# Attention with a gated two-token expert layer on one core: a new order of the first twelve blocks, and turns of small tiles moved between TensorE and the transfer queue

## The chip, the cores and the metric

The kernel runs on one core of one Trainium2 chip. The metric is the device time of one execution in microseconds (us). The time shown for the kernel before is the median of three runs. A profile is one further execution with the hardware profiler on; its span is the time from the first to the last instruction that it records.

## The reference, cut to what matters

There are 2048 tokens of 640 features. x is normalised to xn (layer norm). A 32-head attention with head size 192 runs over a window of the last 512 cached keys and values; its output is projected by wo to s. Beside it two tokens out of 2048 are chosen by a router score, sent through a gated layer, and added into their rows of xn; the result goes through silu and gates s.

```python
xn = _layernorm(x, axis=-1)
# attention: W = 512, Dh = 192, 32 heads, no grouping
q = (xn @ wq).reshape(B, Sq, Hq, Dh).transpose(0, 2, 1, 3)
scores = jnp.einsum("bhqd,bhkd->bhqk", q, k[:, :, Sk - W:]) * (Dh ** -0.5)
o = jnp.einsum("bhqk,bhkd->bhqd", _softmax(scores, axis=-1), v[:, :, Sk - W:])
s = o.transpose(0, 2, 1, 3).reshape(B, Sq, Hq * Dh) @ wo
# expert layer on the C = 2 best tokens
r = xn @ w_r
idx = jnp.argsort(-r, axis=-1)[:, :2]
y = (_silu(x_sel @ w_gate) * (x_sel @ w_up)) @ w_down * _sigmoid(r_sel)
g = _silu(xn + scatter_add(zero, idx, y))
return x + s * g
```

## The kernel before, in words

**Tiling.** Heads are taken in 8 groups of 4 (two pairs a group), tokens in four stretches of 512 (t5 = 0 to 3). A *step* is one pair of heads on one stretch; the steps run over groups, then stretches, then pairs. Each step has two *blocks* of 256 tokens, 128 blocks in all, and each block has two halves of 128 tokens. A block b is made of these tokens, which are also the words of the hand-written order:

- S.b.a, `scores` (line 358): six matmuls into a score tile of two PSUM banks (pool ps_s, two tiles, so the scores of a half need the exps of the half two before it).
- M.b.a, `row_max` (370): a VectorE reduce over the score tile.
- E.b.a, `exps` (375): two exps on ScalarE, into a ring of two blocks, then a transfer that turns p (`pT`). Line 380: blocks in SPLIT are turned in two transfers, one for each half; others in one, after the second half.
- P.b.xy, `o_item` (425): 32 matmuls of turned p with v (line 406), two reciprocals and two scalings to o_sb, one for each of two banks, on VectorE (v) or ScalarE (a) as the two letters say, then a transfer that turns o (`oT`).
- W.k, `w_item` (455): 24 matmuls of turned o with wo (line 447), then two copies or adds of the result into s_acc.
- q.i.c, `q_whole` (302): q of step i, a third c of its columns, with five matmuls and an evacuation on ScalarE (a) or VectorE (v); with a fourth number only one half of the tokens. qa and qb, `q_phase` (323), are the form in two phases that the body uses.

**Layer norm.** `first_*` (252 to 265) and `ln_parts` (486) hold the pieces of layer norm for the first stretch and the others: bn and st are VectorE statistics, sa statistics on ScalarE (`rows`, 501), dev and nw the inverse root, app and ap the application to xn on VectorE, ScalarE or GpSimd (a, v or g). turn.n (`turn_tile`, 279) transposes one 128-token tile of xn on TensorE, 5 transposes into one PSUM bank, and copies it out to xnT on ScalarE or VectorE. xT.3 (line 515) instead turns all four tiles of a stretch with one transfer.

**Loads.** x.t5, k, v, wq and wo are loads issued on SP's queue. ko (`k_order`, 118) is a GpSimd copy of keys into another order; kT (`k_transpose`, 123) is a transfer that turns them; wd (`wo_double`, 148) is a GpSimd copy of wo into the other 64 partitions, which W needs. `group_loads` (604) lays the loads of the next group into lists by block: `loads`, run at the end of a block. Lists bg, mid and end are run at other points of a block.

**Order.** All engines run in the order in which the program issues to them (a manual schedule). The first 12 blocks (HEAD = 12) follow the hand-written list FIRST (588); `first` (528) runs a token, and B.b runs all that the lists hold for block b. In the head, PSUM is two score tiles and four single banks f, which q, turns, P and W share. From block 12 to 125 each block follows BLOCK (910): A S0 M0 W m E0 B S1 M1 P E1 l, where A and B are q phases of the next step, m the list mid, P the item of two blocks before with the list bg between its halves, W the item of six before, and l the lists end and loads. The last two blocks follow LAST.

**Expert layer.** It is spread over the lists (849 to 883). The rows of the two tokens are fetched, normalised (`m_gather`, 731) to xsel, a tile of 2 x 640, and transposed on TensorE in `m_xsT` (755, block 40) to xsT, whose 32 columns are zero beyond the first two. `m_ffn` (762) runs for three parts of 512 columns: matmuls in blocks 41, 49 and 57, the gate in the next block, and `turn` (781) transposes h (128 x 128) on TensorE to hT. `m_down` (804) multiplies with w_down in blocks 62 and 68. `m_sum` (818, block 69) sums the result over partitions through DRAM, and from block 71 GpSimd adds the rows to xn (`m_add`, 831), one 128-token tile every two blocks; ScalarE and VectorE apply the gate from block 75 (`m_gate`, 840).

Of the kernel before, what the change touches and what calls it, by code (L numbers as in the profile page):

```python
# [9 lines left out]
ALU = mybir.AluOpType  # L10
# [3 lines left out]
BF16 = mybir.dt.bfloat16  # L14
# [7 lines left out]
def kernel(ctx, tc, A_x, A_k_cache, A_v_cache, A_wq, A_wo, B_x, B_w_r, B_w_gate, B_w_up, B_w_down, out):  # L22
    nc = tc.nc
    P = 128
# [131 lines left out]
    nc.sync.dma_start(out=x_in[0][:, 2, :], in_=x_v[:, 2, :])  # L156
    nc.scalar.dma_start(out=x_in[0][:, 3, :], in_=x_v[:, 3, :])
# [4 lines left out]
    for _ in range(22):  # L162
        nc.tensor.matmul(warm_ps, lhsT=idle[:, 0:P], rhs=idle, start=True, stop=True)  # L163
# [126 lines left out]
    SPLIT = (NB - 4, NB - 3, NB - 2)  # L290
# [237 lines left out]
    def first(token):  # L528
# [64 lines left out]
    S.3.0 M.3.0 turn.4.a turn.7.v S.3.1 M.3.1 turn.5.a turn.6.v E.3.0 q.2.0.a q.2.1.a P.1.va E.3.1 x.3 wd.2 wd.3 st.2.0 st.2.1 q.2.2.a st.2.2
    S.4.0 M.4.0 q.3.0.a S.4.1 E.4.0 M.4.1 st.2.3 q.3.1.a P.2.va E.4.1 st.2.4 st.2.5 st.2.6 st.2.7
    S.5.0 nw.2.0 M.5.0 q.3.2.a S.5.1 nw.2.1 nw.2.2 E.5.0 M.5.1 nw.2.3 nw.2.4 nw.2.5 nw.2.6 P.3.va E.5.1 ap.10.g ap.8.v sa.3.0.0
    S.6.0 M.6.0 E.6.0 W.0.a S.6.1 M.6.1 ap.9.v ap.11.v P.4.va E.6.1 sa.3.0.1 sa.3.2.0 st.3.6 B.6
    S.7.0 M.7.0 turn.8.v turn.11.v W.1.v turn.9.a turn.10.v S.7.1 M.7.1 E.7.0 P.5.va q.4.0.a q.4.1.a q.4.2.a E.7.1 B.7 sa.3.1.0 sa.3.2.1 st.3.7 sa.3.1.1
# [4 lines left out]
    """.split()

    def group_loads(g, b0, k0, k1, o0, t0, o1, t1, q0, q1, v0, v1, o):
        for c, at in enumerate(k0 + k1):
            loads[b0 + at].append(lambda c=c: k_piece(g, c // 2, c % 2, nc.sync))
        for pr, (a, t) in enumerate(((o0, t0), (o1, t1))):
            loads[b0 + a].append(lambda pr=pr: k_order(g, pr))
            loads[b0 + t].append(lambda pr=pr: k_transpose(g, pr))
        for c, at in enumerate(q0 + q1):  # L610
            loads[b0 + at].append(lambda c=c: wq_piece(g, c // 2, 1 + c % 2, nc.sync))
        for c, at in enumerate(v0 + v1):
            loads[b0 + at].append(lambda c=c: v_piece(g, c, nc.sync))
        for c, at in enumerate(o):
            loads[b0 + at].append(lambda c=c: wo_piece(g, c, nc.sync))
            loads[b0 + at + 2].append(lambda c=c: wo_double(g, c))
# [8 lines left out]
    M = {}  # L625
# [374 lines left out]
```

## Time and profile before

| | us |
|---|---|
| median of 3 runs (803.75 to 805.43) | 804.65 |
| the profiled execution, its own time | 802.92 |
| its span | 801.1 |
| TensorE busy in the span | 781.1 |
| VectorE busy | 589.8 |
| ScalarE busy | 530.3 |
| GpSimd busy | 309.1 |

The granted TensorE clock is 1.00 of full speed. The profile's names are PE for TensorE matmuls, PEld for its weight loads, DVE for VectorE, ACT for ScalarE, POOL for GpSimd, SP for the queue that issues most transfers. A row in the profile gives line, engine, operation and tiles, then how often; "idle before" is time in which the engine stood before such an instruction, and what ended it. Matmuls are pipelined, so the times of their rows overlap; the chain of work that ended last gives each matmul group only the time that it adds. 142.29 MB are transferred in the span, 178 GB/s in the mean, and the queue of SP takes 93.6% of the time of the 16 transfer engines.

### The profile page before, as it was taken

What the parts mean: (1) busy time and instruction counts of PE and PEld (TensorE: products, weight loads), DVE (VectorE), ACT (ScalarE), POOL (GpSimd) and SP (SyncE); (2) the same over time, 40 slices, a digit from 0 to 9 for tenths busy, and PEclk for the clock granted to TensorE, in tenths of its full rate; (3) what the DMA queues carried; (4) which work ended last, traced back from release to release, by engine and by line L of the source; (5) the groups of instructions that cost most, each with busy time, mean ns of one, the idle gap of its engine ahead of it and who ended that gap; (6) DMA issues with size and microseconds to landing.
All of it is one profiled execution on the core that took longest, in us unless ns stands there. A gap on an engine that the chain in (4) does not pass through costs nothing.

```text
span 801.1 us, 26624 instructions
## 1 busy us (share of the span) xinstructions
PE 781.1 (97%) x11354; PEld 576.6 (72%) x11354; DVE 589.8 (74%) x1086; ACT 530.3 (66%) x964; POOL 309.1 (39%) x244
## 2 busy tenths in 40 slices
PE   8799899999999999999999999999999999999997
PEld 4366577777777677777777777777777777777775
DVE  7686588887777767767666677777777777767775
ACT  5678566666666666666666667677767766666662
POOL 1312110011110101001011799949996412564865
PEclk9999999999999999999999999999999999999999
DMA  8998999799999999999998999999999899999993
GB/s 194 189 178 162 197 174 166 148 186 160 188 194 192 171 214 192 196 176 205 198 206 167 173 182 179 169 150 177 174 178 165 145 193 179 189 191 162 177 176 89
DMA packets 445112, 142.29 MB, mean 178 GB/s; under 512 B 412229, under 2 KB 444489, under 8 KB 444993
## 3 DMA queue, kind: packets, MB, share of 16 engines
q1 hardware_dynamic: 435216, 131.18, 93.6%
q10 hardware_dynamic: 8816, 6.88, 3.2%
q0 software_dynamic: 960, 2.52, 1.0%
q8 instruction: 89, 1.46, 0.8%
q14 instruction: 31, 0.25, 0.1%
HBM read 39.98 MB, written 2.62 MB: 53 GB/s over the span
## 4 chain that ended last, share of the span: by engine, by line
PE 89%; DMA 4%; DVE 3%; ACT 2%; issue 1%; POOL 0%; SPq 0%; DVEq 0%; ACTq 0%; POOLq 0%
PE w L447 24%; PE q_ps L340 22%; PE o_ps L406 20%; PE s L367 19%; DMA pT<-pexp 2%; PE q_ps L309 2%; ACT pexp L377 1%; DVE nm L372 1%; PE warm_ps L163 1%; DMA xnT<-xn 1%; DMA wo_g<-in_A_wo_dram 1%; ACT o_sb L420 0%; ACT qT L315 0%; DVE fin_o L475 0%; ACT qT L352 0%
## 5 line engine op out<-in xcount | busy, mean ns | idle before, releaser
L372 DVE TENSOR_REDUCE nm<-s 128x2 f32<-128x1024 f32 x256 | 313.1, 1224 | 135.0 <-PE s L367 130.7
L377 ACT ACTIVATE pexp<-s,nm 128x512 bf16<-128x512 f32 x512 | 324.1, 689 | 96.5 <-DVE nm L372 61.1
L340 PE MATMUL q_ps<-xnT,wq_g 64*128 64x512 bf16 (+1 forms) x2340 | 232.3, 323 | 3.4 <-DMA xnT<-xn 1.5
L447 PE MATMUL w<-wo_g,oT 64*128 64x320 bf16 x3072 | 231.0, 296 | 0.8 <-ACT o_sb L420 0.8
L367 PE MATMUL s<-kT,qT 64*128 64x512 bf16 x1536 | 211.6, 376 | 5.0 <-ACT pexp L377 3.9
L447 PEld LDWEIGHTS <-oT 64*128 64x128 bf16 x3072 | 170.9, 94 | 58.4 <-issue 0.9
L406 PEld LDWEIGHTS <-pT 64*128 64x128 bf16 x4096 | 178.7, 94 | 28.9 <-issue 2.4
L406 PE MATMUL o_ps<-v_sb,pT 64*128 64x193 bf16 x4096 | 197.1, 243 | 0.1
L420 ACT ACTIVATE o_sb<-o_ps,rl 128x192 bf16<-128x192 f32 x256 | 93.8, 418 | 136.7 <-DVE rl L413 132.8
L340 PEld LDWEIGHTS <-wq_g 64*128 64x128 bf16 x2340 | 126.7, 100 | 49.0 <-issue 2.7
L151 POOL COPY wo_g<-wo_g 64x1920 bf16<-64x1920 bf16 x32 | 58.0, 1817 | 219.0 <-DMA wo_g<-in_A_wo_dram 208.2
L367 PEld LDWEIGHTS <-qT 64*128 64x128 bf16 x1536 | 85.1, 94 | 60.1 <-issue 6.4
L470 DVE TENSOR_TENSOR s_acc<-s_acc,w 128x320 f32<-128x320 f32 x192 | 85.0, 484 | 32.4 <-PE w L447 32.3
L352 ACT ACTIVATE qT<-q_ps 128x1024 bf16<-128x1024 f32 x114 | 92.4, 811 | 5.3
L121 POOL COPY k_perm<-k_raw 128x768 bf16<-128x768 bf16 x30 | 25.0, 851 | 139.6 <-DMA k_raw<-in_A_k_cache_dram 108.1
L417 DVE TENSOR_TENSOR o_sb<-o_ps,rl 128x384 bf16<-128x384 f32 x128 | 71.4, 558 | 4.7 <-DVE rl L413 0.4
L836 POOL TENSOR_SCALAR yh<-y_bc,oh 128x640 bf16<-128x640 bf16 x32 | 61.9, 1933 | 3.9 <-DMA y_bc<-y_d 2.3
L837 POOL TENSOR_TENSOR xn<-xn,yh 128x640 bf16<-128x640 bf16 x32 | 44.7, 1397 | 2.7
L413 DVE RECIPROCAL rl<-o_ps 128x2 f32<-128x2 f32 x256 | 30.3, 160 | 16.3 <-PE o_ps L406 9.4
L901 POOL TENSOR_TENSOR s_acc<-s_acc,x_fin 128x640 f32<-128x640 f32 x16 | 22.4, 1399 | 32.0 <-DMA x_fin<-in_A_x_dram 31.5
L833 POOL TENSOR_SCALAR xn<-xn 128x640 bf16<-128x640 bf16 x16 | 29.4, 1838 | 0.8
L478 POOL TENSOR_TENSOR fin_o<-fin_t,s_acc 128x640 bf16<-128x640 f32 x12 | 18.5, 1540 | 17.6 <-DVE fin_t L473 11.0
(138 smaller groups left out, 258.4 us busy)
## 6 DMA issues: line engine op xcount, KB each, us to landing
wo_g<-in_A_wo_dram SPq DMA_DIRECT2D x32, 240.0 KB, 4.2
k_raw<-in_A_k_cache_dram SPq DMA_DIRECT2D x32, 192.0 KB, 3.4
v_sb<-in_A_v_cache_dram SPq DMA_DIRECT2D x32, 192.0 KB, 4.2
wq_g<-in_A_wq_dram SPq DMA_DIRECT2D x14, 288.0 KB, 3.9
wq_g<-in_A_wq_dram SPq DMA_DIRECT2D x14, 192.0 KB, 3.7
x_fin<-in_A_x_dram SPq DMA_DIRECT2D x16, 160.0 KB, 3.5
pT<-pexp SPq DMA_TRANSPOSE x130, 4.8
oT<-o_sb SPq DMA_TRANSPOSE x126, 3.5
```

Source lines behind the costliest of these rows:

```text
L151: nc.gpsimd.tensor_copy(out=grp[g][("wo", pr)][half(1), cs, :], in_=grp[g][("wo", pr)][half(0), cs, :])
L340: mm = nc.tensor.matmul(q_ps[k][:, 0:n] if type(q_ps) is list else q_ps[:, k, 0:n], lhsT=wq[half(r), dc, c:2 * Dh:3], rhs=xnT[half(r), tok ...
L352: nc.scalar.activation(out=out, in_=q_ps[:, :, 0:n], func=ACT.Copy, scale=scale)
L367: nc.tensor.matmul(s_of[b, a][:, r, :], lhsT=qT_of[i][half(r), c, u * P:(u + 1) * P], rhs=grp[g][("kT", pr)][half(r), :, c, :], start=(c = ...
L372: rm = nc.vector.tensor_reduce(out=nm_of[b, a], in_=s_of[b, a], axis=AX.X, op=ALU.max, negate=True)
L377: nc.scalar.activation(out=p_ring[:, b % 2, a, :, hh, :].rearrange("p (x j) e -> p x j e", x=2), in_=s_of[b, a][:, hh, :].rearrange("p (j ...
L406: nc.tensor.matmul(o_of[b][r][:, a, 0:Dh + 1], lhsT=pT_ring[half(r), b % RP, a, k, :], rhs=v_ring[half(r), (g * PAIRS + pr) % RV, k, 0:Dh ...
L417: nc.vector.tensor_tensor(out=o_sb, in0=src, in1=rl[:, r].unsqueeze(2).unsqueeze(3).to_broadcast([P, 2, 3, HK]), op=ALU.mult)
L420: nc.scalar.activation(out=o_sb[:, a], in_=src[:, a], func=ACT.Copy, scale=rl[:, r, a:a + 1])
L447: nc.tensor.matmul(w_ps[r][:, 0:HD], lhsT=oT_ring[half(r), bs[pr] % RT, c, :], rhs=grp[g][("wo", pr)][half(r), c, cs], start=(pr == 0 and ...
L470: nc.vector.tensor_tensor(out=acc, in0=acc, in1=src, op=ALU.add)
L836: nc.gpsimd.tensor_scalar(out=yh, in0=M["y_bc"][:, j, :], scalar1=M["oh"][:, n, j:j + 1], scalar2=None, op0=ALU.mult)
```

## The change

The list FIRST is replaced, and what it names is widened:

- Tile 3 of x goes on SP's queue, not ScalarE's; 13 warm-up matmuls in place of 22.
- The p of blocks 0 to 3 is turned in two transfers each.
- The loads of the second group that fall into the first 12 blocks are tokens of the list of their own (gk keys, go their order, gT their turn, gq, gv, gw loads of wq, v, wo, gd the double); `group_loads` keeps those of block 12 and later. One load of wo moves from block 13 to 14, with its double from 15 to 16.
- xT.3 goes; tiles 12 to 15 are turned on TensorE (turn.12 to turn.15).
- xsel is a tile of 32 x 640, zeroed once, and is turned by a transfer to xsT, issued at the end of block 40; h is turned by a transfer at the end of blocks 43, 50 and 58. The first m_ffn moves from block 41 to 42, the second half of the w_down loads by one block, m_down(1) from 68 to 69 and m_sum from 69 to 70.

```diff
-    nc.sync.dma_start(out=x_in[0][:, 2, :], in_=x_v[:, 2, :])
-    nc.scalar.dma_start(out=x_in[0][:, 3, :], in_=x_v[:, 3, :])
+    for n in (2, 3):
+        nc.sync.dma_start(out=x_in[0][:, n, :], in_=x_v[:, n, :])
...
-    for _ in range(22):
+    for _ in range(13):
         nc.tensor.matmul(warm_ps, lhsT=idle[:, 0:P], rhs=idle, start=True, stop=True)
...
-    SPLIT = (NB - 4, NB - 3, NB - 2)
+    SPLIT = (0, 1, 2, 3, NB - 4, NB - 3, NB - 2)
...
+        elif op == "gk":
+            k_piece(1, n[0] // 2, n[0] % 2, nc.sync)
+        elif op == "go":
+            k_order(1, n[0])
+        elif op == "gT":
+            k_transpose(1, n[0])
...
     FIRST = """
-    bn.1.0 x.1.0 bn.0.0 bn.0.1 v.0 v.1 dev.0 bn.1.1 dev.1 app.0 turn.0.a app.1 bn.3.0 turn.1.a bn.2.0 bn.2.1 dev.2 bn.3.1 kturn.av k.1.0 k.1.1 ko.1 wq.1 x.1.1 dev.3 exp st.1.0 q.0.0.0.v app.2 q.0.1.0.a kT.1 app.3 q.0.2.0.a turn.2.v turn.3.a st.1.1
...
+    v.0 x.1.0 bn.0.0 bn.1.0 x.1.1 bn.1.1 dev.1 bn.0.1 app.1 dev.0 k.1.0 app.0 bn.2.0 turn.0.a bn.3.0 bn.3.1 turn.1.a v.1 kturn.av bn.2.1 wq.1 dev.3 q.0.2.0.a k.1.1 q.0.0.0.v dev.2 v.2 q.0.1.0.a
+    ko.1 app.2 app.3 st.1.0
+    S.0.0 M.0.0 exp x.2 turn.2.a turn.3.a S.0.1 kT.1 M.0.1 st.1.1 E.0.0 st.1.2 wo.0 q.0.1.1.a q.0.0.1.a q.0.2.1.v E.0.1
+    S.1.0 wo.1 st.1.3 st.1.4 S.1.1 M.1.0 st.1.5 E.1.0 q.1.1.a M.1.1 q.1.2.a E.1.1 st.1.6 q.1.0.v st.1.7 nw.1.0
+    S.2.0 nw.1.1 nw.1.2 M.2.0 wo.2 S.2.1 nw.1.3 nw.1.4 nw.1.5 M.2.1 nw.1.6 st.2.0 E.2.0 ap.7.g ap.6.v P.0.vv E.2.1
+    S.3.0 M.3.0 ap.4.a v.3 S.3.1 turn.6.a ap.5.g wd.0 turn.5.a turn.4.v turn.7.v E.3.0 st.2.1 st.2.2 P.1.va M.3.1 wo.3 st.2.3 E.3.1 q.2.1.a q.2.2.v st.2.4 wd.1 q.2.0.v P.2.va
+    S.4.0 M.4.0 S.4.1 E.4.0 x.3 M.4.1 st.2.5 q.3.1.a E.4.1 wd.2 st.2.6 st.2.7 nw.2.0 q.3.2.a nw.2.1 nw.2.2
+    S.5.0 M.5.0 nw.2.3 E.5.0 nw.2.4 q.3.0.v S.5.1 wd.3 nw.2.5 sa.3.0.0 nw.2.6 M.5.1 E.5.1 sa.3.2.0 W.0.v ap.10.g
+    S.6.0 ap.11.g M.6.0 gk.0 E.6.0 ap.9.g ap.8.v W.1.v P.3.av S.6.1 M.6.1 P.4.va
+    S.7.0 st.3.6 E.6.1 turn.10.v turn.11.v turn.9.a turn.8.v sa.3.0.1 M.7.0 S.7.1 E.7.0 gk.1 q.4.2.v gq.0 q.4.1.v q.4.0.a
+    qa.5.0.1 sa.3.1.0
+    S.8.0 M.7.1 go.0 E.7.1 st.3.7 gw.0 sa.3.2.1 sa.3.1.1 nw.3.0 nw.3.1 M.8.0 W.2.v qb.5.0.1 nw.3.2 nw.3.3 nw.3.4 nw.3.5 P.5.av S.8.1 M.8.1 gq.1 nw.3.6 E.8.0 E.8.1 P.6.va ap.15.v
+    qa.5.2 ap.12.v
+    S.9.0 S.9.1 M.9.0 ap.14.g turn.12.v turn.14.v E.9.0 ap.13.g qb.5.2 turn.13.v M.9.1 turn.15.v
+    S.10.0 gT.0 E.9.1 gk.2 gk.3 P.7.vv W.3.v M.10.0 E.10.0 S.10.1 gv.0 P.8.vv W.4.a
+    qa.6.0.1 M.10.1 gd.0
+    S.11.0 E.10.1 M.11.0 B.11 go.1 E.11.0 W.5.v qb.6.0.1 P.9.av q.6.2.v S.11.1 M.11.1 E.11.1 gw.1 gv.1
...
-            group_loads(1, 0, (6, 6), (9, 9), 7, 10, 11, 14, (8, 9), (12, 13), (10, 11), (16, 17), (8, 11, 13, 15))
+            group_loads(1, 0, (6, 6), (9, 9), 7, 10, 10, 14, (8, 9), (12, 13), (10, 11), (16, 17), (8, 11, 14, 15))
...
-        nc.gpsimd.memset(M["xsT"], 0.0)
+        M["xsel"] = M["s"].tile([32, D], BF16, name="xsel")
+        nc.gpsimd.memset(M["xsel"], 0.0)
...
     def m_xsT():
-        xsT_ps = f_tile([P, DC, 2], BF16, "xsT_ps")
-        for dc in range(DC):
-            nc.tensor.transpose(out=xsT_ps[:, dc, :], in_=M["xsel"][:, dc * P:(dc + 1) * P], identity=ident[0:2, 0:2])
-        nc.vector.tensor_copy(out=M["xsT"][:, :, 0:2], in_=xsT_ps)
+        nc.sync.dma_start_transpose(out=M["xsT"], in_=M["xsel"])
...
         def turn():
-            h_ps = f_tile([P, P], BF16, "h_ps")
-            nc.tensor.transpose(out=h_ps, in_=M["h"], identity=ident)
-            nc.vector.tensor_copy(out=M["hT"][:, fb * 4:(fb + 1) * 4, :].rearrange("p c t -> p (c t)"), in_=h_ps)
+            nc.sync.dma_start_transpose(out=M["hT"][:, fb * 4:(fb + 1) * 4, :].rearrange("p c t -> p (c t)"), in_=M["h"])
...
-    bg[40].append(m_xsT)
+    loads[40].append(m_xsT)
...
-    for fb, km in enumerate((41, 49, 57)):
+    for fb, km in enumerate((42, 49, 57)):
...
-        bg[km + 1].append(turn)
+        loads[km + 1].append(turn)
...
-            loads[a + 5 * h].append(m_wd_piece(h, q))
+            loads[a + 6 * h].append(m_wd_piece(h, q))
...
-    bg[68].append(m_down(1))
-    bg[69].append(m_sum)
+    bg[69].append(m_down(1))
+    bg[70].append(m_sum)
```

More of the change, by code (lines that the diff above doesn't have):

```diff
@@ L593 @@
[L593 to L597, printed above, removed]
@@ L607, in group_loads, with at @@
-        for pr, (a, t) in enumerate(((o0, t0), (o1, t1))):
[L608 to L616, printed above, removed]
+        def at(b, f):
+            if b0 + b >= HEAD:
+                loads[b0 + b].append(f)
```

31 lines of the change are left out of this document (20 added, 11 removed).

## The prediction

> **What bounds the kernel now.** I read the busy times and slices first, then windows of the first 12 blocks, TensorE's waits, and the chain that ended last.
>
> ```profile
> PE 781.1 (97%) x11354; PEld 576.6 (72%) x11354; DVE 589.8 (74%) x1086; ACT 530.3 (66%) x964; POOL 309.1 (39%) x244
> ...
> PE   8799899999999999999999999999999999999997
> DMA  8998999799999999999998999999999899999993
> ```
>
> TensorE is full from slice 6 on, so nothing that only rearranges work after about 110 us can pay; what can pay is the head (slices 1 to 5) and TensorE work taken out of the body. The transfer engines are nearly full too, so a transfer's place in SP's queue matters. Busy time by stage (us, then PE, PEld, DVE, ACT, POOL, clock, DMA share, GB/s):
>
> ```profile
> 0.00:39.05 39.05, 31.09 (x253) 16.68 (x254) 27.48 (x67) 23.40 (x44) 7.69 (x13) 1.00 0.93 190
> 39.05:90.05 51.00, 47.09 (x606) 30.01 (x606) 37.13 (x77) 37.49 (x80) 11.04 (x20) 1.00 0.92 179
> 90.05:108.11 18.06, 17.23 (x232) 12.57 (x233) 12.41 (x22) 10.40 (x19) 4.37 (x10) 1.00 1.13 182
> ```
>
> 39.05 is the end of S.4.0 (scores of block 4, first half); at 90.05 block 12 begins on TensorE. What TensorE waited for (total, times, longest):
>
> ```profile
> PE s L367 <- ACT pexp L377: 3.9, 5, 1.0
> PE q_ps L340 <- DMA xnT<-xn: 1.5, 1, 1.5
> PE q_ps L309 <- DVE xnT L283: 1.4, 1, 1.4
> PE tp L282 <- DVE xn L193: 1.3, 1, 1.3
> ...
> PE xsT_ps L758 <- DVE xsel L752: 0.5, 1, 0.5
> ```
>
> Scores wait for exps, which sit in ScalarE's queue behind evacuations of q; that is what a new order can mend. The chain shows one transfer of the head the change deletes, and one delayed behind it:
>
> ```profile
> 74.59 6.92 DMA xnT<-xn
> ...
> 88.34 7.00 DMA pT<-pexp
> ```
>
> **Body, -2.1 us.** In the chain, w's products start every 5.90 us, except around the turns on TensorE:
>
> ```profile
> 253.24 1.64 PE w L447 x24
> 259.14 1.66 PE w L447 x24
> 266.28 1.63 PE w L447 x24
> 272.95 1.63 PE w L447 x24
> 279.13 1.63 PE w L447 x24
> ```
>
> 259.14 to 266.28 is 7.14: 1.24 over 5.90, for xsT with its wait. 272.95 to 279.13 is 6.18: 0.28 for one h turn, and 321.21 to 327.39 and 369.48 to 375.66 give the same. All four go: 1.24 + 3 x 0.28 = 2.1. (The 6.67 between is m_ffn's matmuls, which stay.) The four replacements go on SP behind that block's pT. SP's slot for an o turn is 1.24, and its gap there, 270.2 to 272.25, covers it. No trace row has a 32x640 or 128x128 turn; landing lies between the shortest (3.0, a pT) and longest pT (9.3). I take the pT median, because it waits in the same queue:
>
> ```profile
> pT<-pexp SPq DMA_TRANSPOSE x130, 4.8
> oT<-o_sb SPq DMA_TRANSPOSE x126, 3.5
> ```
>
> Issued at 268.9, xsT lands at 273.7; m_ffn's first product, now a block later, is due near 276.1. Median: hidden. At 9.3 it would cost 2.1, all of this gain. h has 4 blocks or more. m_sum, one block later, shifts y_bc by 5.9; GpSimd finishes tile 0 at 459.6 and ScalarE reads it at 474.7, so 9.2 remains: nothing. The wd loads move with m_down, nothing. The xsel memset on GpSimd, between one and four times the 0.25 row (32x640 has four times the elements per row), has no reader for 28 blocks.
>
> The Trainium skill, "DMA: Bandwidth & Descriptors", section "Rules for kernel authors", says a transfer under 64 KB is mostly overhead and should be coalesced; h is 32 KB. By that rule the turns cost SP and the queues out of proportion to their bytes. No run here shows a turn that small; the sum would still be the same while TensorE does not wait.
>
> **Head, to S.0.0, -0.8.** First transposes start at 8.31, when 22 warm-up matmuls end; their tile was ready at 6.7. Thirteen end near 6.1 (ten at 0.43, three at 0.21). The new order has its first two tiles ready near 7.2 and turns tile 0 then. x tile 3 changes from ScalarE's queue to SP's, 1.5 us later; DVE has other stats first, 0 to -0.6 us of this gain. I take -0.8.
>
> **Head, to S.4.0, +0.6 by itself, but P.2 is then done.** The new order also moves work between engines. Counted over the new list, VectorE gains 3 xnT copies (0.48), 7 whole q evacuations and 3 second halves of o (0.56), and loses 4 applies (0.46). A 128x512 q evacuation on VectorE is in no row: 128x256 takes 0.425, the 128x1024 reduce 1.22, so between these; a 128x384 scaling takes 0.56, 0.13 for 128 elements more, so I take 0.69. Net 1.4 + 4.8 + 1.7 - 1.8 = **+6.1 on VectorE**. ScalarE gains one copy (0.70), loses 7 q (0.60) and 3 o (0.73): **-5.7**. GpSimd gains 4 applies (0.87), idle there. TensorE gains 20 transposes for tiles 12 to 15 (0.06 each): +1.2.
>
> I walked the list by hand with row durations, each instruction when its engine and its inputs are free. So: S.0.0 at 11.9; VectorE, behind app.3 and st.1.0, runs M.0.0 13.0 to 14.2; ScalarE, behind the table and two tile copies, E.0.0 14.7 to 15.9 (was 15.67), q's two evacuations, E.0.1 16.9 to 18.1. VectorE, behind q.0.2.1 and st.1.3 and st.1.4, M.1.0 18.1 to 19.3, and E.1.0 follows at 19.4 (21.37). In the same way E.1.1 at 22.0 (22.99), E.2.0 25.3 (24.94; six small VectorE steps and q.1.0 stand ahead), E.3.0 31.3 (31.10), E.3.1 35.0 (36.85). P.2 needs the bank of q.2.1, which ScalarE empties after E.3.1, at 36.9; P.2 ends at 38.5, S.4.0 at 39.2 (39.05). The transfers give a later bound: x.2 (640 KB) now goes out near 12.6 instead of 26.4, ahead of kT.1 and P.0's turns. The bytes queued up to pT of block 2 are some 6.9 MB; at 189 GB/s that is 36.3, from a start near 2: P.2 from 38.3, S.4.0 at 40.3. I take the middle, 39.7. pT of blocks 0 to 3 in halves adds a slot each:
>
> ```profile
> L383 SPq DMA_TRANSPOSE pT<-pexp x124: 1316/2502/5739, 18.8 to 762.6; - x124
> L381 SPq DMA_TRANSPOSE pT<-pexp x6: 1232/1517/2148, 766.1 to 777.8; - x6
> ```
>
> At 1.5 each SP issues 1.5 + 1.5 + 1.24 + 0.63 = 4.9 us a block against some 6: hidden, and the first half leaves an exp pair (1.27) earlier.
>
> **Head, from S.4.0 to block 12.** TensorE's least work, at chain durations: before, 15 S x 0.65 + 8 P x 1.35 + 6 W x 1.63 + 12 q x 1.08 + 4 tile turns x 0.3 (0.29 in the chain) = 44.5; taken, 89.37 - 39.05 = 50.3, so 5.8 lost, then 0.7 until 90.05. After: one P less, four turns more, 44.4. Lost of the 5.8: xnT's transfer 1.7 goes; the rest I keep, since ScalarE's relief and VectorE's load nearly cancel: 4.1. Bounds: 0 and 15 (each of 16 reduces held 0.69 more). Block 12 begins at 39.7 + 44.4 + 4.1 = 88.2: **-1.85**. The group-1 loads keep their deadlines: k's turn stays in block 10, wo and v come for block 16.
>
> **After block 12.** P.12 was at 108.11, where 90.05 + 5.1 + 2 x 5.9 = 106.95 was possible: 1.2 lost, and 0.7 before. The chain names pT of block 10 (88.34, landing 7.00 later), held behind xnT, k and wq. Now E.10.1 falls near 82, its transfer lands before 90, and S.11.1 covers q.6.2's evacuation. I take half: **-0.9**, bounds 0 and -1.9.
>
> **Sum.** -1.85 - 0.9 - 2.1 = -4.8 (the -0.8 is the walk's start, so inside the first). Span 801.1 becomes 796.3; 1.8 lies around it (802.92 - 801.1), so 798.1 profiled; the median shown is 1.7 above that execution: **799.9**.
>
> **Rivals.**
> *VectorE takes ScalarE's place (slower).* In blocks 4 to 11, reduces of VectorE now stand behind q evacuations and xnT copies; each delays exp, then the scores two ahead, as only two score tiles exist. For: +6.1 us on the engine that is busier over the first 90 us (64.6 against 60.9). Against: VectorE idled 17.1 us before reduces there. Price 0.69 a reduce; the 4.8 gain is eaten by the seventh of 16 and the tenth makes it slower by 0.2%. At twelve: 799.9 + 8.3 = 808.
>
> *Transfers bind early.* For: DMA share 0.93 up to 39.05. x.2's 640 KB, 3.5 us, holds kT.1 and P.0 wholly; 1.1 less than the walk is already taken: +2.4, 802.3.
>
> *The clock falls.* The rows show it rise after 4.3 us of warm-up (weights every 0.43, then ten in 2.04):
>
> ```profile
> 5.43 0.15 PEld L163 LDWEIGHTS <-idle 128*128 128x128 bf16 x1 [0.28 <-issue]
> 5.77 2.04 PEld L163 LDWEIGHTS <-idle 128*128 128x128 bf16 x10 [0.19 <-issue]
> ```
>
> Thirteen leave 0.6 us after it, then a thin stretch; if it fell until the scores, 4.4 us of PE work (0.72 + 0.83 + 1.80 + 1.01) doubles, about half beside copies: +2.2, 802.1. The Trainium skill, "TensorE: Matmul & The Clock Gate", section "Part 1: The HAM clock gate", has the clock halve after an idle window of some 3.4 us and calls the window free-running; the longest gap I see coming is 1.2. Granted clock is 1.00 throughout before.
>
> *The turns do not leave the path.* xsT lands late by the 2.1 above: 802.0.
>
> *The order fits better.* L of 1 instead of 4.1, and all 1.9 after block 12: -4.1, 795.8.
>
> **Chances.** Forecast (797.5 to 802.5) 0.42, better fit 0.16, VectorE 0.22, the three of 802 together 0.20. About 0.2%, 1.6 us, is what a measurement of this kernel can tell from no change: faster is below 803.0, slower above 806.3. The forecast and better fit are faster, and half of the three (0.10): 0.68. Same: their other half and 0.04 of VectorE, 0.14. Slower: 0.18. Range 795.0 to 806.5: it leaves out the best 0.05 and VectorE's worst 0.15.
>
> **What would show it.** Body right: w spacing 5.90 near block 40, no wait for xsT or hT. Head right: block 12's first q at 88.2 (85 to 91), no xnT transfer in the chain, E.3.1 near 35. VectorE rival: scores waiting for pexp and pexp for nm, VectorE unbroken from 60 to 90. Transfers: P.0 or S.2.0 waiting for pT or kT. Clock: under 1.00 before 14 us. The forecast is wrong if block 12 begins after 93.

## The result, and the profile after

| | before | after |
|---|---|---|
| median of 4 runs each | 804.86 us (803.75 to 805.43) | 795.67 us (794.27 to 796.98) |
| ratio after to before, 95% interval | | 0.9887 (0.9867 to 0.9908) |
| the profiled execution, its span | 802.92, 801.1 | 796.98, 795.1 |

The changed kernel is faster by 9.2 us, 1.1%. That lies inside the range of the prediction (795.0 to 806.5), at its lower end; the forecast of 799.9 had 4.8 us of gain. The two profiled executions are 6.0 apart, less than the medians, because the one of before was below all four runs of its table row and the one of after was the highest of its own. So the traces here account for 6.0 us, and the other 3 is taken up with the experiments.

The page of the kernel after, busy times and slices:

```profile
PE 779.8 (98%) x11357; PEld 576.6 (73%) x11357; DVE 597.6 (75%) x1091; ACT 525.9 (66%) x952; POOL 313.8 (39%) x248
...
PE   8899999999999999999999999999999999999997
DMA  9989999799999999999999999999999899999993
```

VectorE went up by 7.8 (6.1 was forecast; some of the 7.8 is steps that stand still, below), ScalarE down by 4.4 (5.7). In TensorE's row slice 2 went from 7 to 8 tenths and slice 5 from 8 to 9, and only the first two slices are below 9 until the last. Two of the three stretches of before, with the columns us, then PE, PEld, DVE, ACT, POOL, clock, DMA share, GB/s:

```profile
0.00:39.05 39.05, 32.60 (x285) 18.05 (x286) 31.52 (x76) 23.39 (x43) 9.58 (x14) 1.00 1.01 215
39.05:90.05 51.00, 50.38 (x645) 32.69 (x645) 42.09 (x84) 35.97 (x73) 15.86 (x30) 1.00 0.93 168
```

From 39.05 to 90.05 TensorE idles 0.6 us where it idled 3.9, and VectorE is busy 42.1 of the 51 without anybody losing by it. (The second stretch after holds almost a block more than before, since block 12 begins in it.) The first stretch moves 215 GB/s where it moved 190. TensorE's own timeline (start, us, instructions of one line in a row) gives the steps of the head, here S.0.0, S.4 and the first q of block 12:

```profile
10.82 1.11 PE L367 MATMUL s<-kT,qT 64*128 64x512 bf16 x6
...
36.83 1.53 PE L367 MATMUL s<-kT,qT 64*128 64x512 bf16 x12
...
84.82 1.26 PE L340 MATMUL q_ps<-xnT,wq_g 64*128 64x512 bf16 x10
```

The row at 36.83 holds both halves of block 4's scores, so S.4.0 ends near 37.5. Block 12 begins at 84.82; before it began at 90.05. And its waits (total, times, longest):

```profile
PE s L367 <- ACT pexp L377: 2.2, 4, 0.8
PE w L447 <- ACT o_sb L420: 2.1, 3, 0.8
...
PE o_ps L406 <- DMA v_sb<-in_A_v_cache_dram: 0.8, 1, 0.8
```

The wait for xnT's transfer (1.5) is gone, scores wait 2.2 for exps instead of 3.9, and a line that was smaller is now second: W waiting for o_sb. Two of those three waits (0.68 and 0.76) are in the blocks whose work was moved, below.

**Where the time went.** The w products are a clock of the kernel: from block 12 on there is one each block. The one of block 13 starts at 92.47 where it started at 98.85, 6.4 us earlier. From there to the end of the span it takes 702.6 where it took 702.3. So the head gained 6.4, more than twice the 2.75 of the prediction, and the body, which was to gain 2.1, gained nothing. These are the rows of w in the chain of work that ended last, of the kernel after, in the blocks whose work was moved:

```profile
252.71 1.66 PE w L447 x24
...
259.29 1.81 PE w L447 x24
...
265.37 1.63 PE w L447 x24
...
272.03 1.67 PE w L447 x24
...
278.72 1.81 PE w L447 x24
```

265.37 to 272.03 is 6.66, m_ffn's products, one block later than before. But 252.71 to 259.29 is 6.58 and 272.03 to 278.72 is 6.69, in place of 5.90 each. No turn runs on TensorE in them any more. (The chain starts such a row where its own part begins; by TensorE's timeline the two spacings are 6.75 and 6.85.) What ran in them is told by the timelines of GpSimd and VectorE:

```profile
255.31 1.78 POOL L151 COPY wo_g<-wo_g 64x1920 bf16<-64x1920 bf16 x1 [18.62 <-DMA wo_g<-in_A_wo_dram]
255.34 1.93 DVE L774 TENSOR_SCALAR xsel<-xg,rs 2x640 bf16<-2x640 bf16 x1
...
274.43 1.78 POOL L151 COPY wo_g<-wo_g 64x1920 bf16<-64x1920 bf16 x1 [11.54 <-DMA wo_g<-in_A_wo_dram]
274.50 1.86 DVE L797 SCALAR_TENSOR_TENSOR th<-th 128x128 f32<-128x128 f32 x1
```

A 2 x 640 scaling takes 1.93 us, and a step on 128 x 128 numbers 1.86. Each begins just after a 1.78 us copy of GpSimd (wo_double) has begun, and ends within 0.2 us of it: 257.27 behind 257.09, 276.36 behind 276.21. Behind them, in the program's order, stand the next reduce, its exp, and the scaling of o that W needs. And the same was there before the change, one instruction earlier. Kernel before, same views:

```profile
261.39 1.78 POOL L151 COPY wo_g<-wo_g 64x1920 bf16<-64x1920 bf16 x1 [17.90 <-DMA wo_g<-in_A_wo_dram]
261.60 1.58 DVE L197 SCALAR_TENSOR_TENSOR rs<-mv,rs 2x1 f32<-2x1 f32 x1
```

Two numbers take 1.58 us. The same kind of step takes 0.14 where no copy runs beside it. So the 7.14 between 259.14 and 266.28, which the prediction put down to the turn of xsT and its wait, may have been mostly this.

### The profile page after: what moved, and what is told of

It reads as the page before. It is cut to its first block, busy times and chain, and to the rows that moved or that the text cites. A ratio compares the mean times of both kernels' runs of the same rounds, so it can differ in the third digit from the quotient of the medians.

```text
span 795.1 us, 26635 instructions
## 1 busy us (share of the span) xinstructions
PE 779.8 (98%) x11357; PEld 576.6 (73%) x11357; DVE 597.6 (75%) x1091; ACT 525.9 (66%) x952; POOL 313.8 (39%) x248
## 3 DMA queue, kind: packets, MB, share of 16 engines
q10 hardware_dynamic: 8672, 6.72, 3.5%
## 4 chain that ended last, share of the span: by engine, by line
PE 89%; DVE 5%; ACT 3%; DMA 2%; issue 1%; SPq 0%; DVEq 0%; ACTq 0%
PE w L447 25%; PE q_ps L340 23%; PE o_ps L406 20%; PE s L367 19%; DVE nm L372 1%; ACT pexp L377 1%; DMA pT<-pexp 1%; PE q_ps L309 1%; DMA v_sb<-in_A_v_cache_dram 1%; ACT o_sb L420 0%; DVE s_acc L470 0%; ACT xnT L283 0%; DMA x_in<-in_A_x_dram 0%; PE tp L282 0%; PE gu_ps L787 0%
## 5 line engine op out<-in xcount | busy, mean ns | idle before, releaser
L420 ACT ACTIVATE o_sb<-o_ps,rl 128x192 bf16<-128x192 f32 x250 | 91.7, 418 | 134.8 <-DVE rl L413 129.5
L417 DVE TENSOR_TENSOR o_sb<-o_ps,rl 128x384 bf16<-128x384 f32 x131 | 73.1, 558 | 4.5
```

The lines of the kernel that those rows point to most:

```text
L417: nc.vector.tensor_tensor(out=o_sb, in0=src, in1=rl[:, r].unsqueeze(2).unsqueeze(3).to_broadcast([P, 2, 3, HK]), op=ALU.mult)
L420: nc.scalar.activation(out=o_sb[:, a], in_=src[:, a], func=ACT.Copy, scale=rl[:, r, a:a + 1])
```

## The experiments

Two theories stood at first. **A**: all of the gain is the head's. The body's turns were cheap, most of the 1.24 was the VectorE step that stands still beside a GpSimd copy, and after the change other steps stand still in the same way. **B**: the body gained its 2.1 as forecast, the head the rest, and the flat sum of the body is another disturbance. Beside these stood theories of what in the head had paid: the shorter warm-up, the turns on TensorE, the halved turns of p, the exchange of evacuations between engines, or only the order. Every ratio is to the kernel before, run beside it on the same chip (medians of before 804.64, 803.98 and 803.64 in the three sets).

### The two halves of the change apart

**e1**: the kernel after, with the expert layer of before.

```diff
-        nc.sync.dma_start_transpose(out=M["xsT"], in_=M["xsel"])
+        xsT_ps = f_tile([P, DC, 2], BF16, "xsT_ps")
+        for dc in range(DC):
+            nc.tensor.transpose(out=xsT_ps[:, dc, :], in_=M["xsel"][:, dc * P:(dc + 1) * P], identity=ident[0:2, 0:2])
+        nc.vector.tensor_copy(out=M["xsT"][:, :, 0:2], in_=xsT_ps)
...
-    for fb, km in enumerate((42, 49, 57)):
+    for fb, km in enumerate((41, 49, 57)):
...
-        loads[km + 1].append(turn)
+        bg[km + 1].append(turn)
```

> The head of the changed kernel (new list, 13 warm-up matmuls, halves of p, tiles 12 to 15 turned on TensorE) with the expert layer of the kernel before (turns of xsel and h on TensorE, m_ffn first in block 41). Theory A: the whole gain is the head's, 6.4 us between the two profiles at P.12, plus what the medians add (9.2 in all); the turns of xsel and h, moved to transfers, give nothing, because two VectorE instructions then run against a GpSimd copy. A expects this kernel within 1 us of the changed one, about 795.7, and the block of the xsel turn 7.1 long again. Rival B: the turns give their 2.1 us and the profile of the changed kernel was an unlucky execution; B expects 797.8.

**e2**: the kernel before, with the expert layer of after; the same edit the other way round.

```diff
-    bg[40].append(m_xsT)
+    loads[40].append(m_xsT)
...
-    for fb, km in enumerate((41, 49, 57)):
+    for fb, km in enumerate((42, 49, 57)):
...
-        bg[km + 1].append(turn)
+        loads[km + 1].append(turn)
```

> The head of the kernel before with the expert layer of the changed kernel (xsel and h turned by transfers, m_ffn first in block 42, m_down and m_sum a block later). Theory A expects no gain, 804 to 805.5; rival B expects 2.1 less than the kernel before, 802.8. Under A a w product waits for o_sb on ScalarE once or twice near blocks 40 to 43, 0.7 us each, behind a VectorE instruction that takes 1.5 to 2 us in place of 0.3 to 0.45.

**e3** and **e4** are the kernels after and before once more, unchanged, for the scatter.

> The changed kernel itself, for a second profile of it beside the others. Both theories: a median of 795.7 within 1 us. Under A, w starts more than 6.6 us apart in block 41 and in block 44 again, each with a VectorE instruction stretched beside a GpSimd copy; under B they are 5.90 apart except for the 6.67 of m_ffn.

> The kernel before itself, for a second profile. Both: a median of 804.9 within 1 us. Under A the small VectorE step before xsel, or xsel itself, is again stretched to 1 us or more by the GpSimd copy of wo, and block 41 of w is about 7.1 long; if the stretch is absent, the turn with its wait should cost about 0.4 in place of 1.24.

| | median us | ratio (95%) | w of block 13 at |
|---|---|---|---|
| e1, head alone | 798.32 | 0.9913 (0.9881 to 0.9945) | 92.20 |
| e2, body alone | 805.83 | 1.0019 (0.9994 to 1.0043) | 98.34 |
| e3, after | 796.60 | 0.9898 (0.9868 to 0.9927) | 92.19 |
| e4, before | 804.87 | 0.9988 (0.9968 to 1.0008) | 99.91 |

The body's edits alone gain nothing: e2 is not faster than before, and its trace has the xsel step at 1.85 us beside a copy of GpSimd. e4 has the stretch of before again: the 2x1 step takes 1.61, and the spacing is 7.16. The head alone gains 6.3 us of 804.64, and its w of block 13 is as early as that of e3. By time e1 is 1.7 slower than e3: A expected it within 1 us of the kernel after, and it came near the 797.8 of B. But most of the two intervals is common to both, so that the times alone don't decide.

The traces do. From w of block 40 to w of block 59 the body's gain of 2.1 would leave 114.4 of the 116.51 of before. It took 116.52 after, 116.25 in e3, and 116.00 in e1, which has the old expert layer. So e1 is not slower than e3 there; it is 1.0 slower ahead of block 40 and 1.6 slower behind block 72, where the two do the same work. And in e1 the copy came after the xsel step and not beside it (timelines of VectorE, GpSimd and TensorE):

```profile
255.90 0.43 DVE L774 TENSOR_SCALAR xsel<-xg,rs 2x640 bf16<-2x640 bf16 x1
256.45 1.78 POOL L151 COPY wo_g<-wo_g 64x1920 bf16<-64x1920 bf16 x1 [19.00 <-DMA wo_g<-in_A_wo_dram]
257.24 0.27 PE L780 MATMUL xsT_ps<-ident,xsel 2*128 2x2 bf16 x5
```

The scaling takes 0.43, xsT's five matmuls wait for nothing, and the spacing of w there is 6.23: the turn of xsT on TensorE costs 0.33 by itself. The same work cost 1.23 in the kernel before; so 0.9 of the 1.24 was the stretched step. e14 (below), with the expert layer of before, agrees: its copy begins at 264.52, behind the 2x1 step (0.14) and xsel (0.43), and its spacing is 6.22. In e3 the copy misses xsel as well, catches h (1.76 us), and one spacing is 6.74. In e2 a step of h begins 0.90 us into the copy of 279.23 and takes 1.02 in place of 0.28: what it pays is the rest of the copy. Which step is caught changes from execution to execution, since the copy starts when its load lands.

### Taking away the copies that collide

**e5**: the kernel after, with the two doubles of wo in question made by a second load from DRAM instead of GpSimd's copy. It adds two transfers and takes two copies away.

```diff
+        if (g, c) in TWICE:
+            eng.dma_start(out=grp[g][("wo", pr)][half(1), cs, :], in_=wo_v[:, c0 + cs.start:c0 + cs.stop, :])
+
+    TWICE = ((3, 0), (3, 1))
...
+        if (g, c) in TWICE:
+            return
```

> The changed kernel, in which the first two wo pieces of group 3 are loaded twice (into both halves of the partitions) in place of being copied by GpSimd; so no GpSimd copy runs beside xsel and the two steps to h. Theory A (the body's gain was eaten because a VectorE instruction stands still while the GpSimd copy of wo runs): xsel takes 0.43 and both steps to h 0.3 each in the profile, w is 5.90 apart in blocks 41 and 44, and the time falls by 0.9 to 1.8 from the changed kernel's 796.6, to about 795.3. Rival C (the stretch comes from something else, such as the transfer of wo landing): the same instructions are stretched again, or W waits as before, and the two extra loads cost 0 to 1 us: 796 to 797.5.

799.32, ratio 0.9942 (0.9922 to 0.9961), where after had 0.9887 and 0.9898: it gave part of the gain back. Yet the steps are as A says once no copy runs, and the waits in the blocks behind them are others (VectorE's, TensorE's and SP's timelines of e5, whose lines are numbered 6 higher):

```profile
255.16 0.43 DVE L780 TENSOR_SCALAR xsel<-xg,rs 2x640 bf16<-2x640 bf16 x1
274.10 0.28 DVE L803 SCALAR_TENSOR_TENSOR th<-th 128x128 f32<-128x128 f32 x1
...
273.73 5.18 SPq L389 DMA_TRANSPOSE pT<-pexp  x1
...
282.00 1.52 PE L412 MATMUL o_ps<-v_sb,pT 64*128 64x193 bf16 x32 [1.09 <-DMA pT<-pexp]
...
284.86 1.26 SPq L807 DMA_TRANSPOSE hT<-h  x1
```

0.43 and 0.28: the cause of the stretch is shown. But P now waits for its turned p, 1.09 and 0.69 us in these blocks (and 1.37 in the head), and the w spacings here are 8.11 and 7.26. The p of the first wait is the one issued at 273.73: its issue holds SP for 5.18 us, where the same turn takes 3.17 in the kernel after, and the next turn of p can only leave behind it, at 281.03. hT's turn is issued at 284.86, after both, so it is not their cause. The two added loads are not needed for it either: e8, e9 and e10 below, whose copies miss all these steps, hold SP for 4.42, 5.36 and 4.44 at the same turn, and so does e13 (4.43), which turns this h on TensorE. All five turn xsT on SP 8 to 9 us earlier. e1 and e14 turn it on TensorE and have 3.13 and 2.30; but e3 and e7 turn it on SP and have 3.07 and 3.58. So xsT's slot may be what makes p late, and it isn't shown. A's time (a gain over after) failed. The collision can't be priced by taking the copy away; its price is the 0.9 from e1 and e14.

### Which part of the head paid

**e7**: the kernel after, but the last stretch of xn is turned by one transfer, as before.

```diff
-    S.9.0 S.9.1 M.9.0 ap.14.g turn.12.v turn.14.v E.9.0 ap.13.g qb.5.2 turn.13.v M.9.1 turn.15.v
+    S.9.0 S.9.1 M.9.0 ap.14.g E.9.0 ap.13.g xT.3 qb.5.2 M.9.1
```

> The changed kernel with tiles 12 to 15 of xn turned by one transfer again, as before (xT.3 behind the last of their applies). Theory D (the transfer of xnT and the p transfers queued behind it cost the old head some 2 to 3 us): block 12 begins 1.5 to 3 later than in the changed kernel, with a wait of q for the xnT transfer, and the time is 798 to 799.5. Rival E (the gain is all from the order of exps and evacuations; the transfer's 7 us are hidden where it now stands): within 1 us, and 1.2 us less TensorE work and 1.9 us less VectorE work even make it 0.5 faster.

802.18, ratio 0.9986 (0.9958 to 1.0013): nearly all of the gain is gone. Block 12 begins at 86.64 and w of block 13 at 94.85, 2.4 later than after. TensorE's waits in e7:

```profile
PE q_ps L340 <- DMA xnT<-xn: 1.6, 1, 1.6
```

The 1.6 is the wait that the turns removed. 2.4 of the head's 6.4 hang on them, as theory D had it. The median lost some 6 us, more than the head's 2.4, and the rest isn't explained: the profiled execution took 807.67, 5.5 above the median, and P waits 3.26 in it for a turned p in one place of the body, at 462.97 (the spacing is 11.01). e12, e13 and e14, with other edits, have a long spacing in the same blocks, 72 and 73 (8.32, 9.58 and 7.35), so no link with the edit of e7 is shown.

**e9**: the kernel after with 22 warm-up matmuls.

```diff
-    for _ in range(13):
+    for _ in range(22):
```

> The changed kernel with 22 warm-up matmuls in place of 13. If the shorter warm-up is worth what the start of the scores moved beyond the tile order, 0.8 to 0.9: the first transposes start at 8.3 in place of 7.2, the first scores near 11.7 in place of 10.8, and the time is 0.5 to 1.0 higher, 797.3. If later waits absorb it: within 0.3. The clock at the start should be the same in both.

798.54, ratio 0.9933 (0.9912 to 0.9953). S.0.0 begins at 12.32, 1.50 later, block 12 at 86.38 and w of block 13 at 94.02, both 1.55 later. In the new order the start of the head passes on whole. Of the 1.5, 0.6 is this execution's: its 22 matmuls took 7.72 us and those of before 7.12 (why, below), so that the nine matmuls themselves are worth about 0.9.

**e12**: the same edit in the kernel before, 13 matmuls for 22.

```diff
-    for _ in range(22):
+    for _ in range(13):
```

> The kernel before with 13 warm-up matmuls and nothing else changed. In the changed kernel the nine matmuls were worth 1.5 us at the sixth w product. Theory G (a start earlier by as much moves the whole head): first transposes at 7.3 in place of 8.3, and block 12 0.8 to 1.5 earlier than 90.05; time 803.3 to 804. Rival (the old head's later waits, on the xnT transfer above all, absorb it): block 12 within 0.4, time 804.6.

806.78, ratio 1.0032 (1.0015 to 1.0049): not faster, even a little slower. TensorE's timeline shows where the earlier start ends:

```profile
6.75 1.01 PE L282 MATMUL tp<-ident,xn 128*128 128x128 bf16 x10 [0.21 <-DVE xn L264]
...
11.67 1.01 PE L282 MATMUL tp<-ident,xn 128*128 128x128 bf16 x10 [1.29 <-DVE xn L264]
12.61 1.47 PE L367 MATMUL s<-kT,qT 64*128 64x512 bf16 x12
```

The first tiles are turned 1.4 us earlier (6.75 for 8.14), but in the old order the turns of tiles 2 and 3 stand ahead of S.0.0 and wait 1.29 for VectorE; S.0.0 begins at 12.61 where it began at 12.68. The new order puts S.0.0 ahead of them. So theory G failed. That the whole became slower by 2.6 us isn't explained by the head: its w of block 13 is at 98.72 (before 98.85). The trace has longer spacings in the body (8.32 at 461.75, 6.72 at 509.79); what ties them to the edit stays open.

**e14**: the kernel before with the turns of tiles 12 to 15 on TensorE in place of the transfer.

```diff
-    qa.5.0.1 S.8.0 B.8 nw.3.0 M.8.0 nw.3.1 nw.3.2 W.2.v qb.5.0.1 nw.3.3 S.8.1 M.8.1 E.8.0 nw.3.4 nw.3.5 nw.3.6 P.6.va E.8.1 ap.13.a ap.15.g ap.14.v ap.12.v xT.3
-    qa.5.2 S.9.0 M.9.0 B.9 W.3.v E.9.0 qb.5.2 S.9.1 M.9.1 P.7.va E.9.1
+    qa.5.0.1 S.8.0 B.8 nw.3.0 M.8.0 nw.3.1 nw.3.2 W.2.v qb.5.0.1 nw.3.3 S.8.1 M.8.1 E.8.0 nw.3.4 nw.3.5 nw.3.6 P.6.va E.8.1 ap.13.a ap.15.g ap.14.v ap.12.v
+    qa.5.2 S.9.0 M.9.0 turn.12.v turn.14.v B.9 W.3.v E.9.0 turn.13.v qb.5.2 turn.15.v S.9.1 M.9.1 P.7.va E.9.1
```

> The kernel before with tiles 12 to 15 turned on TensorE (copies on VectorE, in block 9) in place of the transfer, and nothing else changed. Theory D: block 12 and the sixth w product 2.4 us earlier, as the changed kernel with the transfer put back was 2.4 later; time 802.2, and after block 12 no wait of exps for the turned p of block 10. If the order has to change too for the turns to pay: less than 1 us.

807.11, ratio 1.0044 (1.0023 to 1.0066), slower. The transfer's wait is gone, but the turns come in a place where TensorE waits three times between 71 and 77 us: 0.5 and 0.5 ahead of the turns, for VectorE, and 0.8 where W of step 3 needs a bank that VectorE still has to empty:

```profile
74.07 2.19 PE L447 MATMUL w<-wo_g,oT 64*128 64x320 bf16 x24 [0.79 <-DVE xnT L283]
```

Block 12 begins at 92.98 (before 90.05), w of block 13 at 100.62 (98.85). Of the 1.8, 0.6 is there at the first transposes (8.74 for 8.14; a longer warm-up again). So the same edit that is worth 2.4 in the new order costs about 1.2 in the old one.

**e10**: the kernel after, with all the q evacuations from block 1 on that it had put on VectorE given to ScalarE.

```diff
-    S.1.0 wo.1 st.1.3 st.1.4 S.1.1 M.1.0 st.1.5 E.1.0 q.1.1.a M.1.1 q.1.2.a E.1.1 st.1.6 q.1.0.v st.1.7 nw.1.0
+    S.1.0 wo.1 st.1.3 st.1.4 S.1.1 M.1.0 st.1.5 E.1.0 q.1.1.a M.1.1 q.1.2.a E.1.1 st.1.6 q.1.0.a st.1.7 nw.1.0
...
-    S.3.0 M.3.0 ap.4.a v.3 S.3.1 turn.6.a ap.5.g wd.0 turn.5.a turn.4.v turn.7.v E.3.0 st.2.1 st.2.2 P.1.va M.3.1 wo.3 st.2.3 E.3.1 q.2.1.a q.2.2.v st.2.4 wd.1 q.2.0.v P.2.va
+    S.3.0 M.3.0 ap.4.a v.3 S.3.1 turn.6.a ap.5.g wd.0 turn.5.a turn.4.v turn.7.v E.3.0 st.2.1 st.2.2 P.1.va M.3.1 wo.3 st.2.3 E.3.1 q.2.1.a q.2.2.a st.2.4 wd.1 q.2.0.a P.2.va
...
-    S.7.0 st.3.6 E.6.1 turn.10.v turn.11.v turn.9.a turn.8.v sa.3.0.1 M.7.0 S.7.1 E.7.0 gk.1 q.4.2.v gq.0 q.4.1.v q.4.0.a
+    S.7.0 st.3.6 E.6.1 turn.10.v turn.11.v turn.9.a turn.8.v sa.3.0.1 M.7.0 S.7.1 E.7.0 gk.1 q.4.2.a gq.0 q.4.1.a q.4.0.a
```

(q.3.0 and q.6.2 as well.)

> The changed kernel with its seven whole q evacuations of the head that VectorE does (steps 1 to 6) given back to ScalarE, in the same places of the list: VectorE loses 4.8 us in the first 12 blocks, ScalarE gains 4.2. Theory F (the relief of ScalarE is what shortens the head, since exps stood behind q): block 12 begins 1.5 to 4 later and the time is 798 to 800.5. Rival (VectorE is now the tighter engine, and the evacuations hold up its reduces): block 12 begins 1 to 3 earlier, 794 to 796. In between, within 0.7, the split does not matter, and the order of the other tokens does.

797.05, ratio 0.9920 (0.9899 to 0.9941); block 12 at 85.08 and w of block 13 at 92.72, 0.25 later than after; S.0.0 began 0.5 later already (11.31), ahead of the edit. Which of the two engines empties q hardly matters.

**e8**: the kernel after, p of blocks 0 to 3 turned in one transfer each.

```diff
-    SPLIT = (0, 1, 2, 3, NB - 4, NB - 3, NB - 2)
+    SPLIT = (NB - 4, NB - 3, NB - 2)
```

> The changed kernel with p of blocks 0 to 3 turned in one transfer each, as before. If the halves matter (P.0, P.1 and P.2 of the changed kernel already wait up to 0.8 for a transfer each): P.0 starts 1 to 2 later, S.4.0 and block 12 follow by 0.5 to 2, time 797.5 to 799. If four more slots of SP cost as much as they give: block 12 begins within 0.3 of 84.8 and the time is within 0.7 of the changed kernel's 796.6.

797.28, ratio 0.9915 (0.9886 to 0.9945); w of block 13 at 93.00, 0.5 later, from an S.0.0 that began 0.2 earlier (10.59). So the halves are worth 0.5 to 0.8 in the head, below what the times can tell.

### A version that might beat both

**e13**: the kernel after, with xsel made at the end of block 40, the gate of the first m_ffn a block later, the first h turned on TensorE again, and v of the fourth head loaded a block earlier.

```diff
-            spot(29 + b).append(it)
+            (end[40] if b == 11 else spot(29 + b)).append(it)
...
-        mid[km + 1].append(act)
-        loads[km + 1].append(turn)
+        mid[km + (2 if fb == 0 else 1)].append(act)
+        (bg[km + 2] if fb == 0 else loads[km + 1]).append(turn)
```

> The changed kernel with three moves away from what it was seen to wait for: the making of xsel goes to the end of block 40 and the gate of the first m_ffn to block 44 (both out of the GpSimd copy of wo), the first h is turned on TensorE in block 44 (0.27) since SP's slots of blocks 43 to 46 are full, and the load of v for head 3 goes one block earlier (P.2 waited 0.8 for it). If these waits are what ate the body's gain: no small VectorE step stretched, blocks 40 to 47 at 5.90 but for 0.77 of m_ffn and 0.3 of the turn, and the time 0.8 to 2 below the changed kernel, 794.6 to 795.8. If the transfers of p run late there for another reason: blocks 45 and 46 lose 1 us or more again, and the time is 796 to 798.

797.42, ratio 0.9891 (0.9862 to 0.9920): not to be told from after. The edits did what they say: no VectorE step is stretched, the 0.8 us wait for v is gone, and w of block 13 is at 91.36, 1.1 earlier than after. The profiled execution, the slowest of its six (800.37), gave it back in the body: spacings of 7.14 (282.81) and 6.31 (289.12) around the turn of h, which waits 0.90 for a bank that ScalarE empties late, its exps having waited 2.29 for the late turn of p, and 9.58 at 462.79, where P waits 3.02 for its turned p.

## Why the prediction was right, and where its sizes were wrong

**Sign and range** were right; 9.2 us were gained where 4.8 were forecast. What came is the split of no rival: 6.4 from the head and nothing from the body, where the sum had 2.75 and 2.1, and "The order fits better" 6.9 and 2.1. That the median lies beside the 795.8 of that rival is luck: it has 792.2 for the span (796.3 - 4.1), the profiled one is 795.1, and the difference is made up by the 3 us that the medians show beyond the two traces.

A second pair of executions, e4 and e3, has these 3 us: their spans differ by 9.3, 7.7 up to w of block 13 and 1.6 behind it (704.3 and 702.7). But executions of the old head differ among themselves: w of block 13 is at 98.34 (e2), 98.85 (before) and 99.91 (e4), and the first transposes at 7.76, 8.14 and 8.88. Most of that is the warm-up. Its weights are loaded every 0.43 us at first and every 0.20 later, the change comes at 4.96 in e2, 5.77 in before and about 7.1 in e4, and so the 22 matmuls take 6.74, 7.12 and 7.85:

```profile
1.19 7.85 PE L163 MATMUL warm_ps<-idle 128*128 128x512 bf16 x22 [1.19 <-DVE idle L160]
```

In the new head 13 of them end before the first tile is ready, and w of block 13 lies between 92.19 and 92.47 in four executions (after, e1, e3, e5). So the head's gain is 5.9 to 7.7 by the pair that is taken, 6.4 for the two profiles shown. Behind the head the two executions of before differ by 2.0 (702.3 and 704.3), and no edit is shown to cause that.

**"Body, -2.1 us"** is the step that failed. Three terms of it:
- *"259.14 to 266.28 is 7.14: 1.24 over 5.90, for xsT with its wait."* The turn is 0.33 of it (e1; 0.32 in e14). The rest is the 2x1 step that stood still beside GpSimd's copy. The wait that the prediction quoted, xsT_ps for xsel (0.5), was true and not the turn's own: xsel stood behind that step.
- *"and m_ffn's first product, now a block later"* was costed at nothing. m_ffn's gate moved with it, into the next copy of wo: 0.95 in the profiled execution after (spacing 6.85). Nothing in the prediction names a copy beside it.
- *"The four replacements go on SP behind that block's pT ... Median: hidden."* This held in the kernel after: the landings were as taken (xsT 4.6, h 4.4 to 5.3; forecast 4.8), and no wait of TensorE is put down to them. The spacing of block 49 is 6.93, 0.26 over what it was, but that is ahead of the second turn of h, which SP issues at 325.90: m_ffn's products wait 0.18 at 312.09 for ScalarE to empty q, and e1, which turns h on TensorE, has 6.81 there. In other executions of the new body (e5, e9) TensorE waited for xsT (0.5) or P for a late p; the sum had no term for what a fuller queue does to the transfers behind, and whether xsT's slot is the cause stays open.

As a sum over the blocks from 40 to 58, in spacings by TensorE's timeline: gone 1.23 + 3 x 0.27 = 2.04, which is the prediction's 2.1; added 0.85 + 0.95 + 0.26 = 2.06. It is 0.0, and the 116.52 from w of block 40 to w of block 59, where it was 116.51, agrees. The 2.1 was not out of reach: in e7, where the copies miss all these steps and no p is late, the same stretch takes 114.99, 1.5 less. So the step that failed is the one that took every us above 5.90 for the turns' own, and the steps' new places for free, without looking at what else ran there.

**"Head, to S.0.0, -0.8"** was 1.9 (10.82 for 12.68). The transposes began where the walk had them (7.23; forecast 7.2). The 13 matmuls ended at 6.73 and not near 6.1, since their weights came every 0.43 to the last; that cost nothing, as the tile was not ready. The clock did not fall behind them, over a gap of 0.50 us: ten transposes take 0.73 (0.72 before) and fifteen q matmuls 1.80 (1.80). (The column of the granted clock can't tell: it has 1.00 for the slow first 5 us too.) What the walk lost is the next step. In the old order ten turns of tiles 2 and 3 took 0.9 between q and S.0.0 (11.74 to 12.68); the new list has them behind it, at 11.87. e12 shows this is not an effect of the warm-up: without the new order the same 13 matmuls give 0.07.

**"Head, to S.4.0, +0.6"**: from that start all steps of the walk came early by 0.9 to 2.0: E.0.0 13.76 (14.7), E.1.0 18.34 (19.4), E.2.0 23.96 (25.3), E.3.0 29.37 (31.3), E.3.1 33.28 (35.0); S.4.0 ended at 37.5 (39.7). Of these 2.2, 1.1 is the late start and 1.1 the walk and the bound that was averaged into it. The bound of the transfers used 189 GB/s, from the stage of before; with 215, which this stage reached, the 6.9 MB end at 34.1, and P.2 began at 35.55. A rate that was read off while the queues were not always full (a DMA share of 0.93, now 1.01) is no ceiling. The 0.69 for a 128x512 evacuation on VectorE was right (0.64 to 0.69).

**"Head, from S.4.0 to block 12"**: 84.82 - 37.5 - 44.4 leaves 2.9 lost, where 4.1 was taken and 6.5 was before (the 5.8, and 0.7 up to 90.05). e7 gives what the prediction took as 1.7 for xnT's transfer: 1.8 at block 12, 2.4 with what follows.

**"After block 12, -0.9"**: P.12 is at 101.72, 84.82 + 5.1 + 2 x 5.9 = 101.72. Nothing is lost where 1.2 was: 1.2 came and 0.9 was taken. The prediction took half of 1.9, the 1.2 and the 0.7 ahead of block 12; but its 88.2 for block 12 leaves that 0.7 out already, so the 0.7 is in the sum one and a half times. Without it the sum is 0.35 smaller, some 800.2.

**What the head's 6.4 is made of**, by what w of block 13 loses if one part is undone: the warm-up 1.55 (e9), the turns on TensorE 2.4 (e7), the halves of p 0.5 (e8), the engines of q 0.25 (e10). That is 4.7, or 4.1 if the warm-up counts 0.9; the other 1.7 to 2.3 is the order itself and its loads, which were not undone one by one. Each is one execution, and four of the same head differ by 0.3, so the 0.25 is not told from nothing. The parts are not worth this apart from the order: two of them alone in the old order gave -0.1 and +1.8 us at that point (e12, e14; +1.2 without the longer warm-up), and three executions of the old head differ by 1.6.

**The rivals.** *VectorE takes ScalarE's place*: refuted. VectorE was the busier engine of the stage, 42.1 of 51 us, and giving its evacuations back to ScalarE changed 0.25 us (e10); the wait of the scores for exps fell instead of rising. *Transfers bind early*: only the 0.8 wait for v, and P.0's 0.4 for pT. *The clock falls*: refuted by the rows named above. *The turns do not leave the path*: its price, no gain from the body, came true by a mechanism that it did not name, the stretched steps: xsT was not late. That an edit of the head pays only together with the order was named nowhere; e12 and e14 show it.

## What to carry to other kernels

When a spacing grows around an operation, look at the instruction ahead of the wait on each engine, and compare its duration with its other rows, before charging the operation: a 0.14 us step that takes 1.58 is the cause, not the turn behind it. A step that moves to another block meets other neighbours there, so look at what runs beside its new place as well. That a moved transfer lands in time doesn't yet show that it is free: look at what its queue issues behind it. And an earlier start is worth something only if the order lets the rest follow, so the order and the start are to be walked together.

## What the runs showed of the hardware that was not expected

Some VectorE steps that start while GpSimd copies 64x1920 bf16 (1.78 us) end only when the copy does: 0.14 became 1.58 (two numbers), 0.28 became 1.86 (128x128 f32), 0.43 became 1.93 (2x640 bf16), and 0.28 became 1.02 where the step began halfway (e2), each ending within 0.2 us of the copy, and e5, without the copies, has 0.43 and 0.28 again. It is a full stop and not a sharing of bandwidth, as the size of the step makes no difference. It is not every step: those that read a matmul's result from PSUM run on. In the kernel after, beside the copy from 312.19 to 313.97, the copy of gu_ps at 312.87 takes 0.42, as it does without one (270.11), and the reciprocals of o_ps take their 0.24. The Trainium skill, "SBUF — State Buffer", section "SBUF: two separate sides", says so: VectorE and GpSimd have a pair of ports in common, "an exclusive lock, not a bandwidth split", that whoever starts first holds for its whole instruction, against steps of VectorE with two inputs in SBUF or in a two-port mode. The traces agree on the stop, on its length, and on the steps that read PSUM; which of the two conditions held for the xsel step, which reads one tensor, they don't show. Had the prediction weighed that sentence against the 1.78 us copies of wo, the 1.24 could have been seen in two parts.

A turn of h (128x128 bf16, 32 KB) takes as long as one of p, which has sixteen times the bytes (four exps of 128x512 bf16): in the kernel after it landed in 4.4 to 5.3 us, a turn of p in 5.0 (the median of 134, 14 of them halves), and it took SP 1.27 to 1.88 to issue. That agrees with the rule that the prediction weighed, of the Trainium skill, "DMA: Bandwidth & Descriptors", section "Rules for kernel authors": a small transfer is mostly overhead. The prediction's sum left this out since TensorE did not wait for h, and in the kernel after no wait of TensorE is put down to it.
